# One layer of decoding: whole-matrix loads of wq and w3, and a final copy in two parts

## The chip, the cores and the metric

The kernel runs on one core of one Trainium2 chip. The metric is the device time of one execution in microseconds (us). A core has five engines that concern us: TensorE (PE; its weight loads are shown as PEld), VectorE (DVE), ScalarE (ACT), GpSimd (POOL) and SyncE (SP), each with an instruction stream of its own, and 16 DMA engines that move data between HBM and the on-chip memory SBUF. PSUM is the memory into which TensorE writes its products. An instruction that needs another engine's result, or a transfer, waits on a semaphore, and what stands behind it in the same stream waits with it.

## The reference

One token for each of 4 sequences passes through attention over a cached window and a gated feed-forward block, both with a residual and a layernorm in front:

```
x: 4 x 1024;  wq: 1024 x 4096;  wo: 4096 x 1024
k, v: the last 2048 positions of 4 sequences x 4 heads x 8192 positions x 128
w1, w3: 1024 x 3584;  w2: 3584 x 1024         (all bfloat16)

q   = layernorm(x) @ wq                       # 32 query heads, 8 to each k/v head
p   = softmax(q k^T / sqrt(128));  o = p v
h   = x + o @ wo
out = h + (silu(layernorm(h) @ w1) * (layernorm(h) @ w3)) @ w2
```

Nearly all of the work is reading weights and cache once: the profile counts 55.59 MB read from HBM.

## The kernel before, in words

All weights and the cache pass through one tile, `ring` (line 88), of 160 KiB in each of the 128 partitions. It is no ring of equal slots: a list, `plan` (lines 110 to 125), gives for each load its kind, its function and the address at which it is put. Addresses are written in KiB. `load_rows` (line 90) loads some rows of a weight matrix with one DMA (a wq row takes 8 KiB in a partition, a wo or w2 row 2 KiB, a w1 or w3 row 7 KiB), `load_kv` (line 96) two sequences of k or v with one DMA each. All of these DMAs go out on SyncE's queue.

`load_next(n)` (line 129) takes the next n entries of the plan, issues their DMAs at that place of the program, and puts the resulting views into `loaded`, from which the matmuls take them. The framework sees the program in this order. A load waits for those reads of its address range that stand before it in the program, and a read waits for the last load of its range that stands before it. Which plan entry a call of `load_next` issues therefore depends only on how many entries were taken by the calls ahead of it. Before the change the calls issue:

| call, line | entries | KiB in the tile |
|---|---|---|
| start, 138 | wq rows 0 to 3; wq rows 4 to 7; k 0, 1; k 2, 3; v 0, 1 | 0-32; 32-64; 64-96; 96-128; 128-160 |
| in the q loop at kc = 3, 223 | v 2, 3 | 0-32 |
| in the scores, half of the units, 275 | wo (32 rows) | 32-96 |
| in the p v loop at b = 1, 334 | w1 (8 rows) | 96-152 |
| in the p v loop at b = 3, 334 | w3 rows 0 to 3 | 0-28 |
| in the wo loop at i = 11, 361 | w3 rows 4 to 7 | 28-56 |
| after the wo loop, 362 | w2, 17 rows | 56-90 |
| in the w1 loop at k = 3, 411 | w2, 7, 3 and 1 rows | 90-104; 104-110; 110-112 |

The stages follow each other in the program:

- x is loaded (line 137), normalised and transposed. The q product (lines 210 to 221) runs 64 matmuls (L215), 8 for each of 8 wq rows.
- Scores: keys are transposed on TensorE (L263), copied by VectorE and ScalarE in turn (L267, L269), and multiplied with q (L248). Softmax, then the product with v (L326).
- The wo product (L353): 32 rows, 4 matmuls each, into `y_ps`. Residual and layernorm on VectorE (L366 to L391), with a small matmul for the sums over partitions (L375). `y2_ps` is begun with the residual (L395).
- `gate_up` (line 398) multiplies with w1 into `g_ps` and with w3 into `u_ps` (both L403, 64 matmuls each). Between the two stand the exponential on ScalarE (L415) and add, reciprocal and product on VectorE (L416 to L419), which make the gate `gs`.
- `hg` (L422) is gate times `u_ps`; it is transposed (L425) and multiplied with w2's 28 rows, 4 matmuls each, into `y2_ps` (L433).
- The tail: one copy from PSUM (L443) and one store (L444), both on ScalarE.

The framework's scheduler may exchange neighbouring independent instructions on an engine; within that the engines follow the program.

Of the kernel before, what the change touches and what calls it, by code (L numbers as in the profile page):

```python
# [10 lines left out]
P = 128  # L11
# [8 lines left out]
def kernel(  # L20
# [13 lines left out]
    nc = tc.nc  # L34

    B, _, D = A_x.shape
# [12 lines left out]
    x_flat = A_x.flatten_outer_dims()  # L49
    out_flat = out.flatten_outer_dims()  # L50
# [14 lines left out]
    JG = 4  # L65
    QD = P // JG
    RS = QD // B
# [13 lines left out]
    RQ = 4  # L81
    BS = 2
    wq_v = A_wq.rearrange("(p i) n -> p (i n)", i=KC)
    wo_v = A_wo.rearrange("(p i) n -> p (i n)", i=IO)
    w1_v = B_w1.rearrange("(p i) n -> p (i n)", i=KC)
    w3_v = B_w3.rearrange("(p i) n -> p (i n)", i=KC)
# [9 lines left out]
    def load_kv(at, src, b):  # L96
# [11 lines left out]
    N_Q, N_F = Hq * Dh, F  # L108
    KIB = 512
    plan = [  # L110
        ("wq", load_rows, (0, wq_v, N_Q, 0, 4)),
        ("wq", load_rows, (32 * KIB, wq_v, N_Q, 4, 4)),
        ("k", load_kv, (64 * KIB, A_k_cache, 0)),
        ("k", load_kv, (96 * KIB, A_k_cache, 2)),
        ("v", load_kv, (128 * KIB, A_v_cache, 0)),
        ("v", load_kv, (0, A_v_cache, 2)),
        ("wo", load_rows, (32 * KIB, wo_v, D, 0, 32)),
        ("w1", load_rows, (96 * KIB, w1_v, N_F, 0, 8)),
        ("w3", load_rows, (0, w3_v, N_F, 0, 4)),
        ("w3", load_rows, (28 * KIB, w3_v, N_F, 4, 4)),  # L120
        ("w2", load_rows, (56 * KIB, w2_v, D, 0, 17)),
        ("w2", load_rows, (90 * KIB, w2_v, D, 17, 7)),
        ("w2", load_rows, (104 * KIB, w2_v, D, 24, 3)),
# [5 lines left out]
    def load_next(n=1):  # L129
        for _ in range(n):  # L130
            if cursor[0] < len(plan):
                kind, f, args = plan[cursor[0]]
                loaded.setdefault(kind, []).extend(f(*args))
                cursor[0] += 1

    x_sb = act.tile([B, D], BF16)
    nc.scalar.dma_start(out=x_sb[:], in_=x_flat)
    load_next(5)

    ident = const.tile([P, P], BF16)  # L140
    make_identity(nc, ident[:])
# [5 lines left out]
    for j in range(JG):  # L147
        nc.scalar.dma_start(
            out=x_q[QD * j : QD * (j + 1) : RS, :], in_=x_flat[:, j * CG : (j + 1) * CG]
# [7 lines left out]
    for c in range(2):  # L157
# [8 lines left out]
        out=xn[:], in0=x_sb[:], scalar1=mv[:, 0:1], scalar2=rstd[:, 0:1],  # L166
# [4 lines left out]
    for kc in range(KC):  # L171
# [15 lines left out]
        out=perm[:].rearrange("p (h dq) -> p h dq", dq=JG),  # L187
        in_=ident[:].rearrange("p (dq h) -> p h dq", dq=JG),
# [12 lines left out]
    for j in range(2, JG):  # L201
        nc.vector.tensor_tensor(
            out=same[:, 0, :], in0=same[:, 0, :], in1=ident[:, j * QD : (j + 1) * QD], op=ALU.add
# [6 lines left out]
    for kc in range(KC):  # L210
        wq_t = loaded["wq"][kc]
        for hf in range(CQ // 512):
            for g in range(JG):
                c0 = g * CQ + hf * 512
                nc.tensor.matmul(  # L215
                    q_ps[QD * g : QD * g + B, hf * 512 : (hf + 1) * 512],
                    lhsT=xnT[:, kc, :],
                    rhs=wq_t[:, c0 : c0 + 512],
                    start=(kc == 0),
                    stop=(kc == KC - 1),  # L220
                )
        if kc == RQ - 1:
            load_next()
    q_sb = act.tile([P, CQ], BF16)
    nc.vector.tensor_single_scalar(out=q_sb[:, :512], in_=q_ps[:, :512], scalar=qscale, op=ALU.mult)  # L225
    nc.scalar.mul(out=q_sb[:, 512:], in_=q_ps[:, 512:], mul=qscale)
# [1 line left out]
    for r in range(REP):  # L228
        nc.tensor.transpose(out=qt_ps[:, r, :], in_=q_sb[:, r * Dh : (r + 1) * Dh], identity=ident[:])
    nc.vector.tensor_copy(  # L230
        out=qz[:, :, : Hkv * QD].rearrange("p b (g z) -> p b g z", g=Hkv)[:, :, :, :REP],
        in_=qt_ps[:].rearrange("p r (g x) -> p x g r", g=Hkv)[:, :B, :, :],
# [24 lines left out]
    for u, (b, n) in enumerate(units):  # L257
        k_v = loaded["k"][b]
        kT = ktpool.tile([P, NJ, P], BF16, tag="kT")
        for t in range(NJ // TB):  # L260
            kt_ps = psA.tile([P, TB, P], BF16, tag=f"kt{nt % 4}")
            for jj in range(TB):
                nc.tensor.transpose(  # L263
                    out=kt_ps[:, jj, :], in_=k_v[:, n * NJ + t * TB + jj, :], identity=ident[:]
# [21 lines left out]
        out=Pm[:], in_=scores_ps[:], func=ACT.Exp, bias=nmax[:], scale=1.0, accum_out=rsum[:]  # L286
# [6 lines left out]
    for c in range(NSB):  # L293
# [4 lines left out]
        for g in range(Hkv):  # L298
            if g % 2 == 0:
                nc.vector.tensor_scalar(  # L300
                    out=z[:, :, g, :], in0=pt_ps[:], scalar1=mask[:, g : g + 1], scalar2=None, op0=ALU.mult
# [10 lines left out]
        out=Dm[:], in0=ident[:].rearrange("p (g b r) -> p b g r", g=Hkv, b=B),  # L312
# [35 lines left out]
    y2_ps = psB.tile([P, CG], FP32, tag="y2")  # L348
    g_ps = psB.tile([P, 2, 512], FP32, tag="g")
    u_ps = psB.tile([P, 2, 512], FP32, tag="u")  # L350
    for i in range(IO):
# [34 lines left out]
        out=hn[:], in0=h1[:], scalar1=tot[:, 0:1], scalar2=rstd2[:, 0:1],  # L386
# [5 lines left out]
        out=hnT[:].rearrange("p k x -> p (k x)"), in_=hn[:].rearrange("q (c k) -> q k c", k=KC)  # L392
# [5 lines left out]
    def gate_up(kind, out_ps):  # L398
# [27 lines left out]
        out=hgT[:].rearrange("p i x -> p (i x)"),  # L426
        in_=hg[:].rearrange("q s c -> q (s c)").rearrange("q (c i) -> q i c", i=IF),
# [12 lines left out]
            )  # L440

    res = act.tile([P, CG], BF16)
    nc.scalar.copy(out=res[:], in_=y2_ps[:])  # L443
    nc.scalar.dma_start(out=out_flat.rearrange("b (j c) -> j b c", j=JG), in_=res[0:P:RS, :])  # L444


# [28 lines left out]
```

## Time and profile before

| what | value |
|---|---|
| median of 3 runs | 138.12 us (138.05 to 138.14) |
| the profiled execution's own time | 138.12 us |
| its span, first to last instruction | 136.3 us |
| TensorE matmul busy | 67.9 us (50%) |
| VectorE busy | 42.6 us (31%) |
| ScalarE busy | 31.0 us (23%) |
| SyncE's DMA queue: bytes, share of 16 engines' time | 55.58 MB, 95.3% |
| mean rate | 409 GB/s |
| mean granted TensorE clock | 0.792 of full speed |

Busy time of an engine is the sum of its instructions' durations; shares are of the span. The profile's slices cut the span into 40 equal parts of 3.4 us; each digit is the busy share in tenths. The chain of waits starts at the last instruction and goes back, at each step to what released it. A line of the timeline gives start, length, engine, line of the kernel, operation, output and inputs, a count where several are merged, and in brackets how long the engine stood idle before and what ended that. "SPq" and "ACTq" are instructions that issue a DMA or wait, on the engine's queue. The profile cuts the names `w1`, `w3` and `w2` to `w`, and `y_ps` stands for `y2_ps` too.

### The profile page before, as it was taken

The numbers are of one execution on the slowest core, as the hardware profiler recorded it, in microseconds if no ns is written. First come the engines' busy times: TensorE is split into PE (matmuls) and PEld (weight loads), VectorE is DVE, ScalarE is ACT, GpSimd is POOL, SyncE is SP. The second block draws the span as 40 slices with busy tenths as digits, with TensorE's granted clock in tenths as the row PEclk, the third lists the DMA queues.
The fourth block names the chain that finished last, engine by engine and source line by source line (L and its number), as shares of the span: only waits on it lengthen the run. The fifth ranks groups of instructions, "written<-read, shape, count | busy, mean of one in ns | idle before, by whom it ended". The sixth has DMA issues, their size and how long they took to land.

```text
span 136.3 us, 2302 instructions
## 1 busy us (share of the span) xinstructions
PE 67.9 (50%) x1035; PEld 42.9 (31%) x1035; DVE 42.6 (31%) x73; ACT 31.0 (23%) x36; POOL 1.7 (1%) x8
## 2 busy tenths in 40 slices
PE   0101803698989889105259538830096440900960
PEld 0100201274656565001149427610043210300840
DVE  6440000244444444609940030160000695070000
ACT  0400000155555646092944000000003300000001
POOL 5000000000000000000000000000000000000000
PEclk9999999999999999965555865897557777555577
DMA  5999899999999999997988989989799999989960
GB/s 156 462 462 443 385 413 418 423 447 423 428 437 409 437 437 423 435 582 341 538 385 365 524 365 442 459 353 522 328 412 463 434 437 447 429 388 409 426 261 5
DMA packets 2662, 55.75 MB, mean 409 GB/s; under 512 B 312, under 2 KB 344, under 8 KB 604
## 3 DMA queue, kind: packets, MB, share of 16 engines
q1 hardware_dynamic: 2592, 55.58, 95.3%
q8 instruction: 8, 0.13, 0.3%
q10 hardware_dynamic: 60, 0.02, 0.1%
q14 instruction: 2, 0.02, 0.0%
HBM read 55.59 MB, written 0.01 MB: 408 GB/s over the span
## 4 chain that ended last, share of the span: by engine, by line
DMA 58%; PE 21%; ACT 13%; DVE 5%; issue 1%; SPq 0%; ACTq 0%
DMA ring<-in_B_w_dram 42%; DMA ring<-in_A_wq_dram 16%; PE kt_ps L263 9%; ACT kT L269 6%; PE scores_ps L248 5%; ACT z L304 3%; PE q_ps L215 2%; PE g_ps L403 2%; DVE rmax L280 2%; ACT Pm L285 2%; PE OT_ps L326 2%; DVE pT L294 1%; DVE z L300 1%; ACT L285 1%; DVE q_sb L225 1%
## 5 line engine op out<-in xcount | busy, mean ns | idle before, releaser
L269 ACT COPY kT<-kt_ps 128x1024 bf16<-128x1024 bf16 x16 | 15.8, 1014 | 12.0 <-PE kt_ps L263 12.0
L263 PE MATMUL kt_ps<-ident,ring 128*128 128x128 bf16 x256 | 16.4, 219 | 0.0
L263 PEld LDWEIGHTS <-ring 128*128 128x128 bf16 x256 | 14.3, 98 | 5.0 <-issue 4.9
L267 DVE COPY kT<-kt_ps 128x1024 bf16<-128x1024 bf16 x16 | 11.1, 691 | 15.2 <-PE kt_ps L263 15.2
L215 PE MATMUL q_ps<-ring,xnT 128*4 128x512 bf16 x64 | 6.7, 596 | 12.0 <-DMA ring<-in_A_wq_dram 12.0
L403 PEld LDWEIGHTS <-hnT 128*32 128x32 bf16 x128 | 5.3, 137 | 23.1 <-issue 20.5
L248 PE MATMUL scores_ps<-kT,qz 128*32 128x512 bf16 x64 | 9.9, 609 | 3.1 <-ACT kT L269 3.1
L326 PE MATMUL OT_ps<-z,ring 128*128 128x32 bf16 x256 | 7.4, 185 | 6.7 <-ACT z L304 5.0
L403 PE MATMUL u_ps<-ring,hnT 128*32 128x448 bf16 x64 | 6.3, 572 | 8.3 <-DMA ring<-in_B_w_dram 8.3
L403 PE MATMUL g_ps<-ring,hnT 128*32 128x448 bf16 x64 | 5.4, 525 | 9.0 <-DMA ring<-in_B_w_dram 9.0
L433 PE MATMUL y_ps<-ring,hgT 128*32 128x256 bf16 x112 | 5.7, 370 | 8.4 <-DMA ring<-in_B_w_dram 8.3
L326 PEld LDWEIGHTS <-ring 128*128 128x128 bf16 x256 | 7.3, 103 | 7.4 <-issue 7.4
L433 PEld LDWEIGHTS <-hgT 128*32 128x32 bf16 x112 | 4.4, 129 | 10.3 <-issue 6.1
L215 PEld LDWEIGHTS <-xnT 128*4 128x4 bf16 x64 | 2.1, 116 | 16.2 <-issue 15.9
L353 PE MATMUL y_ps<-ring,o 128*32 128x256 bf16 x128 | 5.8, 365 | 2.0 <-DMA ring<-in_A_wo_dram 2.0
L443 ACT CAST res<-y_ps 128x256 bf16<-128x256 f32 x1 | 0.4, 372 | 26.5 <-PE y_ps L433 26.5
L304 ACT ACTIVATE z<-pt_ps,mask 128x512 bf16<-128x512 f32 x8 | 5.3, 687 | 3.5 <-DVE z L300 3.5
L225 DVE TENSOR_SCALAR q_sb<-q_ps 128x512 bf16<-128x512 f32 x1 | 0.7, 690 | 17.2 <-PE q_ps L215 17.2
L353 PEld LDWEIGHTS <-o 128*32 128x32 bf16 x128 | 4.8, 130 | 3.8 <-issue 3.1
L300 DVE TENSOR_SCALAR z<-pt_ps,mask 128x512 bf16<-128x512 f32 x8 | 5.5, 740 | 1.2 <-ACT z L304 0.8
L296 PE MATMUL pt_ps<-pT,perm 128*128 128x512 bf16 x4 | 2.4, 607 | 6.8 <-DVE pT L294 6.8
L417 DVE RECIPROCAL eg<-eg 128x896 f32<-128x896 f32 x1 | 5.8, 5753 | 0.0
(73 smaller groups left out, 40.5 us busy)
## 6 DMA issues: line engine op xcount, KB each, us to landing
ring<-in_A_wq_dram SPq DMA_DIRECT2D x2, 4096.0 KB, 16.8
ring<-in_A_k_cache_dram SPq DMA_DIRECT2D x4, 2048.0 KB, 25.5
ring<-in_A_v_cache_dram SPq DMA_DIRECT2D x4, 2048.0 KB, 40.2
ring<-in_B_w_dram SPq DMA_DIRECT2D x1, 7168.0 KB
ring<-in_B_w_dram SPq DMA_DIRECT2D x2, 3584.0 KB, 28.6
ring<-in_B_w_dram SPq DMA_DIRECT2D x1, 4352.0 KB
ring<-in_B_w_dram SPq DMA_DIRECT2D x1, 1792.0 KB
ring<-in_B_w_dram SPq DMA_DIRECT2D x1, 768.0 KB
```

Source lines behind the costliest of these rows:

```text
L215: nc.tensor.matmul(q_ps[QD * g : QD * g + B, hf * 512 : (hf + 1) * 512], lhsT=xnT[:, kc, :], rhs=wq_t[:, c0 : c0 + 512], start=(kc == 0), ...
L248: nc.tensor.matmul(scores_ps[QD * g : QD * (g + 1), n * 512 : (n + 1) * 512], lhsT=qz[:, b, g * QD : (g + 1) * QD], rhs=kT_v[:, g, :, :], ...
L263: nc.tensor.transpose(out=kt_ps[:, jj, :], in_=k_v[:, n * NJ + t * TB + jj, :], identity=ident[:])
L267: nc.vector.tensor_copy(out=kT[:, t * TB : (t + 1) * TB, :], in_=kt_ps[:])
L269: nc.scalar.copy(out=kT[:, t * TB : (t + 1) * TB, :], in_=kt_ps[:])
L300: nc.vector.tensor_scalar(out=z[:, :, g, :], in0=pt_ps[:], scalar1=mask[:, g : g + 1], scalar2=None, op0=ALU.mult)
L304: nc.scalar.mul(out=z[:, :, g, :], in_=pt_ps[:], mul=mask[:, g : g + 1])
L326: nc.tensor.matmul(OT_ps[:, b, :], lhsT=loaded["v"][b][:, j, :], rhs=PTz[j // NJ][:, (j % NJ) * B + b, :, :], start=(j == 0), stop=(j == J ...
L353: nc.tensor.matmul(y_ps[QD * j : QD * (j + 1), :], lhsT=o4[:, i, :, :].rearrange("p b s -> p (b s)"), rhs=loaded["wo"][i][:, j * CG : (j + ...
L403: nc.tensor.matmul(out_ps[QD * j : QD * (j + 1), hf, :HF], lhsT=hnT[:, k, :], rhs=loaded[kind][k][:, c0 : c0 + HF], start=(k == 0), stop=( ...
L417: nc.vector.reciprocal(out=eg[:], in_=eg[:])
L433: nc.tensor.matmul(y2_ps[QD * j : QD * (j + 1), :], lhsT=hgT[:, i, :], rhs=loaded["w2"][i][:, j * CG : (j + 1) * CG], start=False, stop=(i ...
```

## The change

wq and w3 become one plan entry, and so one DMA, each. The first call of `load_next` takes 4 entries instead of 5, the call inside the q loop moves behind it, and the other calls stay where they are. The load of x is split into two halves by columns. The final copy is split: VectorE copies columns 0 to 159 and SyncE's queue stores them, ScalarE copies columns 160 to 255 and stores them from its own queue.

```diff
     plan = [
-        ("wq", load_rows, (0, wq_v, N_Q, 0, 4)),
-        ("wq", load_rows, (32 * KIB, wq_v, N_Q, 4, 4)),
+        ("wq", load_rows, (0, wq_v, N_Q, 0, 8)),
         ("k", load_kv, (64 * KIB, A_k_cache, 0)),
         ("k", load_kv, (96 * KIB, A_k_cache, 2)),
         ("v", load_kv, (128 * KIB, A_v_cache, 0)),
         ("v", load_kv, (0, A_v_cache, 2)),
         ("wo", load_rows, (32 * KIB, wo_v, D, 0, 32)),
         ("w1", load_rows, (96 * KIB, w1_v, N_F, 0, 8)),
-        ("w3", load_rows, (0, w3_v, N_F, 0, 4)),
-        ("w3", load_rows, (28 * KIB, w3_v, N_F, 4, 4)),
+        ("w3", load_rows, (0, w3_v, N_F, 0, 8)),
         ("w2", load_rows, (56 * KIB, w2_v, D, 0, 17)),
...
     x_sb = act.tile([B, D], BF16)
-    nc.scalar.dma_start(out=x_sb[:], in_=x_flat)
-    load_next(5)
+    for c0, c1 in ((0, 512), (512, D)):
+        nc.scalar.dma_start(out=x_sb[:, c0:c1], in_=x_flat[:, c0:c1])
+    load_next(4)
...
-        if kc == RQ - 1:
-            load_next()
+    load_next()
...
     res = act.tile([P, CG], BF16)
-    nc.scalar.copy(out=res[:], in_=y2_ps[:])
-    nc.scalar.dma_start(out=out_flat.rearrange("b (j c) -> j b c", j=JG), in_=res[0:P:RS, :])
+    out_v = out_flat.rearrange("b (j c) -> j b c", j=JG)
+    CV = 160
+    nc.vector.tensor_copy(out=res[:, :CV], in_=y2_ps[:, :CV])
+    nc.scalar.copy(out=res[:, CV:], in_=y2_ps[:, CV:])
+    nc.sync.dma_start(out=out_v[:, :, :CV], in_=res[0:P:RS, :CV])
+    nc.scalar.dma_start(out=out_v[:, :, CV:], in_=res[0:P:RS, CV:])
```

## The prediction

> **What bounds the kernel now.** I read the row of DMA slices first, then the chain of waits, then the timeline of the second half, then the sync engine's queue alone. The page's row says that the transfers never pause between start and end:
>
> ```profile
> DMA  5999899999999999997988989989799999989960
> ```
>
> The chain in order of time says which transfers the end hangs on (start, length, what):
>
> ```profile
> 1.16 21.35 DMA ring<-in_A_wq_dram
> ...
> 73.22 25.79 DMA ring<-in_B_w_dram
> ...
> 101.59 31.37 DMA ring<-in_B_w_dram
> ...
> 133.01 0.32 PE y_ps L433 x4
> ...
> 133.35 0.37 ACT res L443
> ```
>
> The timeline shows TensorE starting each product when its weights land (start, length, idle before, releaser in brackets):
>
> ```profile
> 82.25 5.76 PE L353 MATMUL y_ps<-ring,o 128*32 128x256 bf16 x128 [2.04 <-DMA ring<-in_A_wo_dram]
> ...
> 99.06 5.44 PE L403 MATMUL g_ps<-ring,hnT 128*32 128x448 bf16 x64 [9.01 <-DMA ring<-in_B_w_dram]
> ...
> 107.50 3.13 PE L403 MATMUL u_ps<-ring,hnT 128*32 128x448 bf16 x32 [3.00 <-DMA ring<-in_B_w_dram]
> ...
> 115.98 3.17 PE L403 MATMUL u_ps<-ring,hnT 128*32 128x448 bf16 x32 [5.34 <-DMA ring<-in_B_w_dram]
> ...
> 126.30 3.82 PE L433 MATMUL y_ps<-ring,hgT 128*32 128x256 bf16 x68 [7.14 <-DMA ring<-in_B_w_dram]
> 130.55 1.11 PE L433 MATMUL y_ps<-ring,hgT 128*32 128x256 bf16 x28 [0.43 <-DMA ring<-in_B_w_dram]
> 132.38 0.92 PE L433 MATMUL y_ps<-ring,hgT 128*32 128x256 bf16 x16 [0.71 <-DMA ring<-in_B_w_dram]
> ```
>
> So the landings are wo 82.2, w1 99.06, w3 107.50 and 115.98, w2 126.30, 130.55, 132.38, 133.01. 7.34 MB of w1 in 16.8 us is 437 GB/s: one unbroken stream. It stays unbroken because each issue waits only for a read that is done before the stream is empty; the sync queue's issues are
>
> ```profile
> 73.22 0.33 SPq L93 DMA_DIRECT2D ring<-in_B_w_dram  x1
> ...
> 78.84 0.33 SPq L93 DMA_DIRECT2D ring<-in_B_w_dram  x1
> ...
> 85.04 0.33 SPq L93 DMA_DIRECT2D ring<-in_B_w_dram  x1
> ...
> 87.73 0.33 SPq L93 DMA_DIRECT2D ring<-in_B_w_dram  x1
> ```
>
> that is w1, both halves of w3 and the 17 rows of w2, then the three short w2 pieces at 100.7 to 101.6, all well before 126.3.
>
> **What the Trainium skill says.** "DMA: Bandwidth & Descriptors", section "Anatomy of one DMA": the DMA engines don't wait on semaphores; the issuing sequencer waits, before it issues, and everything after it in its stream waits too. The trace agrees: the second half of w3 is issued at 85.04, only when wo's rows have been read. "TensorE: Matmul & The Clock Gate", section "What's actually happening": after some 3.4 us idle the array runs at half rate until about 3.4 us of work have passed. The trace agrees: w2's first 68 matmuls take 56 ns each, the next 28 take 40. "PSUM — Partial Sum Buffer", section "Terms": ScalarE and VectorE must not use one bank's quadrant together. No line of before shows that; it bears on the split copy.
>
> **The change, part by part.**
>
> *What is handed out when.* The calls that issue loads take the next plan entry. Up to w1 the two removed items cancel (one wq entry less, the first call takes 4 instead of 5). w3 then is one entry, so each later entry comes one call early: all of w3 at b = 3, ahead of the wo loop; w2's 17 rows at i = 11 of that loop; w2's 7 rows after it, ahead of w1's loop. The ranges overlap: w3 takes 0 to 56 KiB, wo's rows 0 to 11 lie in 32 to 56 and rows 12 to 28 in 56 to 90, exactly where w2's 17 rows go; w2's 7 rows (90 to 104) cover w1's row 0 and the start of row 1. A load that stands ahead of a read of its range in the program is taken as what is read. So the reads wait for the later load. The compiled order has it:
>
> ```
> L351 Ldweights o4_130 [waits DMAHW7,DMAHW1,DVE]
> L351 Matmult y_ps<-ring,o4_130 32x256 [waits DMAHW2]     (row 12)
> L401 Ldweights hnT [waits DMAHW3]                        (first g_ps)
> ```
>
> Before, the first of them waited for semaphore 7 (wo) alone and the other two had no such wait. The eight semaphores go round in order of issue: 1 is w3, 2 the 17 rows, 3 the 7 rows. (In this part the changed kernel multiplies with w3's and w2's bytes in place of wo's rows 0 to 28, and with w2's in part of w1's rows 0 and 1; number and shapes of the matmuls stay.)
>
> *wq as one DMA.* The first 32 q matmuls (3.58 us at 13.05) no longer run while the second half comes: all 64 start at 22.55. That delays the scores by up to 3.2 us, less what the compiled order gets back by transposing keys ahead of q. v's second half is issued near 29, with some 9 MB still queued (wq, k and v's first half are 21 MB, and 409 GB/s, the page's mean, moves about 11.5 by then). w1 is issued near 76 instead of 73.22, and the stream holds until wo lands at 82.2: hidden. If it came after 79.4 (82.2 less the start-up below) the stream would break, one for one. k's third load waits for wq's semaphore until 22.5, when two k loads are still queued. Cost 0.
>
> *The x load in two.* One more issue of up to 0.57 us on ScalarE's queue; q's inputs were ready at 7.2 and wait for wq till 22.55. Cost 0.
>
> *The stream from wo on.* w3 is issued when wo lands, 82.2 (its new wait), w2's 17 rows right behind; w1 covers both until 99.06. So w1 lands at 99.06, w3 at 115.98, the 17 rows at 126.30, as before. Now TensorE comes after them:
> - 115.98: wo's rows 0 to 11, 48 matmuls, 2 to 2.7 us; then row 12 waits for 126.30. Queued behind it is all of the rest of TensorE's work, and for that DVE's layernorm.
> - 126.30: 80 matmuls, cold. 61 x 56 ns make the first 3.4 us; the warm price is (5.76 - 3.4) / 67 = 35 ns from L353 and 40 from w2's 28: I take 37, 19 x 37 = 0.7. Ends at 130.4.
> - The sync queue holds w2's 7 rows until wo's last rows are read, 130.4: the stream is empty from 126.3. Start-up: wq's first half landed 12.32 us after its issue at 0.73, the second 9.5 after the first, so 2.8; plus 4.25 for the bytes (126.30 to 130.55). Landing: 137.45. The fixed cost of about 2 us that the same DMA section gives is the lower end.
> - Layernorm: y's end at 88.01 to the next product's weights at 92.32, 4.31: 134.7.
> - The compiled order puts 37 u matmuls first: 34 cold at 99 ns (3.17 / 32), 3 warm: 3.6, to 138.3. The wait for the 7 rows has passed by then.
> - g: 64 at the warm price (5.44 - 3.4) / 30 = 68 ns: 4.35, to 142.65. The other 27 u are hidden behind what follows; so are w2's last pieces, issued when w1's rows 1 and 2 are read, near 139.
> - g's end to gs's end: 104.50 to 114.45, 9.95 (table load 1.28, exponential 0.92, add 0.63, reciprocal 5.75, product 1.09). Before, this lay under w3's transfer; now nothing covers it. 152.6.
> - hg and its transpose: 119.20 to 122.08, 2.9: 155.5.
> - w2: 112 matmuls, nothing to wait for: 61 x 56 + 51 x 38 = 5.35: 160.85.
>
> *The tail.* Before, y's end to the span's end is 136.3 - 133.33 = 2.97. The compiled order makes ScalarE's part wait for VectorE's. VectorE's 160 columns: 0.29 for 128 (L336) and 0.42 for 256 (L366), so 0.32; ScalarE's 96: 0.19 for 128 (L320), so about 0.15, and two hand-overs. The later store is issued 0.57 after y instead of 0.42: +0.15. Two smaller stores may gain 0.3 or cost 0.5.
>
> Sum: 160.85 + 3.12 = 164.0 of span. The profiled execution was 138.12 us with a span of 136.3; the 1.82 around it stays: 165.8. The median shown is 138.12 as well.
>
> **The rivals.**
> - *The new waits are already met* (a semaphore counts an earlier load): then only the tail is left, 138.12 + 0.15 = 138.3, not slower by what can be told here. For it: the order shows no counts. Against: semaphores 1 and 2 were used by k in both kernels, and only the changed one waits. It decides if y starts at about 82. 4%.
> - *Only w3 is waited for*, the 17 rows not: y 115.98 to 121.75, layernorm to 126.05, the 7 rows land unbroken at 130.55, g to 135.0, then 9.95 + 2.9 + 5.35 + 3.12 + 1.82: 158.1. Against: the separate wait at row 12. 3%.
> - *The clock stays cold* in y, u, g and w2: +0.4, +2.05, +0.9: 169.2. For it: in 116 to 119.2 and 119.2 to 126.3 the granted clock was 0.50. Against: L353 and L403 did speed up midway. 8%.
> - *Warm throughout*: y -1.1, g -0.85 (then the 7 rows' landing holds it), w2 -1.1: 162.8. Long idle times stand against it. 3%.
>
> **How the numbers follow.** 82% for 165.8, with 164 to 168.8 of its own (clock phases, start-up 2.0 to 3.5, tail). Range 163.8 to 169.2. Slower by over 0.2% (about what a measurement of this kernel can tell from none) 96%, same 3%, faster 1%.
>
> **What would show it.** y's matmuls starting near 116 and pausing until 126; a hole of some 7 us in the DMA row after 126 with the 7 rows issued at 130; the reciprocal on the chain; a second half that ends on engines, not on DMA. A y that starts at 82, or a stream that still runs until 133, would make the forecast wrong.

## The result, and the profile after

The changed kernel takes 166.44 us (median of 6 runs, 165.73 to 167.3) against 138.13 (138.05 to 138.3) of the kernel before: a ratio of 1.2056, 95% interval 1.2017 to 1.2095. The profiled execution took 166.42 us with a span of 164.6. It is not the same layer any more: TensorE runs matmuls of the same number and shapes, but nowhere multiplies with wo's rows 0 to 28 or with a part of w1's rows 0 and 1.

The row of DMA slices of the changed kernel's page, each slice now 4.1 us, is no longer full to the end:

```profile
DMA  7998979999999999899899999999991280700000
```

Up to slice 30 it looks as before. Slices 31 and 32 are nearly empty, slices 33 and 35 are filled once more, and after slice 35 nothing moves: over the last eighth of the span engines work alone. The same bytes are moved, 55.75 MB, but at a mean of 339 GB/s over the span instead of 409. The chain of waits, in order of time (start, length, what), says what the end now hangs on:

```profile
41.31 41.10 DMA ring<-in_A_wo_dram
...
82.87 43.56 DMA ring<-in_B_w_dram
...
126.48 3.85 PE y_ps L351 x79
...
134.60 3.91 PE u_ps L401 x28
138.52 3.73 PE g_ps L401 x47
...
145.22 5.76 DVE eg L415
...
155.15 5.73 PE y_ps L431 x58
...
161.26 0.24 ACT res L444
```

Before, a DMA stood on this chain until 132.97. Now the last DMA on it ends at 126.44 (w2's 17 rows), and what it releases is the second part of the wo product. After it come the rest of that product, layernorm, the products with w3 and w1, the reciprocal and w2's product, one after the other, for 38 us. The timeline of the changed kernel shows where TensorE stood until then:

```profile
82.81 0.27 PE L339 MATMUL o_ps<-oT,perm 128*128 128x128 bf16 x1 [0.73 <-DVE oT L337]
...
116.28 2.75 PE L351 MATMUL y_ps<-ring,o 128*32 128x256 bf16 x48 [33.21 <-issue]
...
126.48 3.82 PE L351 MATMUL y_ps<-ring,o 128*32 128x256 bf16 x80 [7.44 <-DMA ring<-in_B_w_dram]
...
134.60 3.91 PE L401 MATMUL u_ps<-ring,hnT 128*32 128x448 bf16 x37 [2.27 <-DVE hnT L389]
137.94 4.27 PE L401 MATMUL g_ps<-ring,hnT 128*32 128x448 bf16 x64
...
155.15 5.69 PE L431 MATMUL y_ps<-ring,hgT 128*32 128x256 bf16 x112 [11.80 <-DVE hgT L423]
```

wo's product, one run of 128 at 82.25 before, is now cut into 48 and 80, at row 12, and starts at 116.28, where the second half of w3 landed before (115.98). The first wait of 33.2 us is put down to "issue": the semaphores are waited for by the weight load in front of the matmul, and the profile names no releaser there. The second is named as a DMA of a feed-forward weight. Of the three that the wo product could wait for, w3 must have landed by 116.28 and w2's 7 rows were not issued before 130.34, so it is w2's 17 rows. The sync engine's queue shows these issues:

```profile
82.50 0.80 SPq L93 DMA_DIRECT2D ring<-in_B_w_dram  x2
...
130.34 0.33 SPq L93 DMA_DIRECT2D ring<-in_B_w_dram  x1
...
140.00 0.80 SPq L93 DMA_DIRECT2D ring<-in_B_w_dram  x2
```

w3 and the 17 rows go out together when wo lands; the 7 rows go out when wo's product is done. In between the stream stands still. The same stretch before and after (the figures are the length, the busy time and number of instructions of TensorE's matmuls and weight loads, VectorE, ScalarE and GpSimd, the granted TensorE clock, the busy share of the DMA engines, and GB/s):

```profile
126.30:130.50 4.20, 3.82 (x68) 3.04 (x68) 0.00 (x0) 0.00 (x0) 0.00 (x0) 0.50 0.98 416
126.30:130.50 4.20, 3.82 (x80) 3.06 (x79) 0.10 (x1) 0.00 (x0) 0.00 (x0) 0.62 0.01 4
```

### The profile page after: what moved, and what is told of

It reads as the page before. It is cut to its first block, busy times and chain, and to the rows that moved or that the text cites. A ratio compares the mean times of both kernels' runs of the same rounds, so it can differ in the third digit from the quotient of the medians.

```text
span 164.6 us, 2303 instructions
## 1 busy us (share of the span) xinstructions
PE 65.3 (40%) x1035; PEld 41.4 (25%) x1035; DVE 42.8 (26%) x74; ACT 31.0 (19%) x36; POOL 1.7 (1%) x8
## 2 busy tenths in 40 slices
DMA packets 2402, 55.75 MB, mean 339 GB/s; under 512 B 320, under 2 KB 344, under 8 KB 600
## 4 chain that ended last, share of the span: by engine, by line
DMA 65%; PE 20%; DVE 8%; ACT 3%; issue 1%; SPq 0%; DVEq 0%; ACTq 0%
DMA ring<-in_B_w_dram 26%; DMA ring<-in_A_wo_dram 25%; DMA ring<-in_A_wq_dram 13%; PE kt_ps L261 4%; DVE eg L415 4%; PE q_ps L214 3%; PE y_ps L431 3%; PE u_ps L401 2%; PE y_ps L351 2%; PE g_ps L401 2%; ACT kT L267 2%; PE scores_ps L246 2%; DVE hgT L423 1%; ACT L413 1%; DVE hg L420 1%
## 5 line engine op out<-in xcount | busy, mean ns | idle before, releaser
L351 PE MATMUL y_ps<-ring,o 128*32 128x256 bf16 x128 | 6.6, 391 | 40.7 <-issue 33.2
L261 PE MATMUL kt_ps<-ident,ring 128*128 128x128 bf16 x256 | 17.1, 220 | 0.0
L246 PE MATMUL scores_ps<-kT,qz 128*32 128x512 bf16 x64 | 10.5, 609 | 2.6 <-ACT kT L267 2.6
L214 PE MATMUL q_ps<-ring,xnT 128*4 128x512 bf16 x64 | 5.7, 538 | 9.4 <-DMA ring<-in_A_wq_dram 9.4
L401 PE MATMUL u_ps<-ring,hnT 128*32 128x448 bf16 x64 | 5.4, 483 | 2.3 <-DVE hnT L389 2.3
L401 PEld LDWEIGHTS <-hnT 128*32 128x32 bf16 x128 | 4.0, 119 | 6.6 <-issue 2.9
L171 PE MATMUL tp_ps<-ident,xn 4*128 4x4 bf16 x8 | 0.7, 199 | 12.7 <-DVE xn L164 12.7
```

Of the source, the lines that this page charges most:

```text
L214: nc.tensor.matmul(q_ps[QD * g : QD * g + B, hf * 512 : (hf + 1) * 512], lhsT=xnT[:, kc, :], rhs=wq_t[:, c0 : c0 + 512], start=(kc == 0), ...
L246: nc.tensor.matmul(scores_ps[QD * g : QD * (g + 1), n * 512 : (n + 1) * 512], lhsT=qz[:, b, g * QD : (g + 1) * QD], rhs=kT_v[:, g, :, :], ...
L261: nc.tensor.transpose(out=kt_ps[:, jj, :], in_=k_v[:, n * NJ + t * TB + jj, :], identity=ident[:])
L351: nc.tensor.matmul(y_ps[QD * j : QD * (j + 1), :], lhsT=o4[:, i, :, :].rearrange("p b s -> p (b s)"), rhs=loaded["wo"][i][:, j * CG : (j + ...
L401: nc.tensor.matmul(out_ps[QD * j : QD * (j + 1), hf, :HF], lhsT=hnT[:, k, :], rhs=loaded[kind][k][:, c0 : c0 + HF], start=(k == 0), stop=( ...
```

## The experiments

Each timed run stands beside runs of the kernel before on the same chip (138.14 us median; 138.23 for the two runs with x alone and wq alone). The ratios can differ by 0.1% from the quotient of the medians, so a tenth of a us between two runs says little.

**Where the 28 us are: w3 in a place where nothing is overwritten.** The changed kernel, with one call taken out:

```diff
-        if b % BS == BS - 1:
+        if b == BS - 1:
             load_next()
```

> The changed kernel without the call of load_next at b = 3, so that w3 (still one DMA) is issued at i = 11 of the wo loop and all of w2 where the kernel before had it; nothing is loaded over rows that are still to be read. Theory (the 28 us come from reads that wait for a load handed out one call early): w3 lands near 116, its 64 matmuls end near 121.5 instead of 119.2, hg and its transpose near 124.4, still ahead of w2's landing at 126.3; the stream runs unbroken to 133 and only the new tail is left: 138.3 to 139.0 us. Rival (a matrix as one DMA costs time in itself, since its matmuls start only at the end): at least the 3.2 us of half of w3's matmuls on top, 141 us or more, or a stream slower than 430 GB/s.

138.89 us, ratio 1.0043 (1.0031 to 1.0055). The timeline shows all 64 matmuls of w3 after the one landing, and w2's product still waiting for its own transfer:

```profile
116.14 5.80 PE L401 MATMUL u_ps<-ring,hnT 128*32 128x448 bf16 x64 [11.28 <-DMA ring<-in_B_w_dram]
121.99 1.09 DVE L420 TENSOR_TENSOR hg<-u_ps,gs 128x896 bf16<-128x896 f32 x1 [7.18 <-PE u_ps L401]
123.11 1.70 DVE L423 STREAM_TRANSPOSE hgT<-hg 128x896 bf16<-128x896 bf16 x1
...
126.40 3.82 PE L431 MATMUL y_ps<-ring,hgT 128*32 128x256 bf16 x68 [4.46 <-DMA ring<-in_B_w_dram]
```

The later matmuls shorten the last idle time from 7.14 to 4.46 us and cost nothing. So one large DMA is not what is slow; the place of its issue in the program is. That is shown, since this kernel has every other edit of the change and loses 0.75 us by the medians (0.6 by the ratio), not 28.3.

**The other way round: w3 alone.** The kernel before, with

```diff
-        ("w3", load_rows, (0, w3_v, N_F, 0, 4)),
-        ("w3", load_rows, (28 * KIB, w3_v, N_F, 4, 4)),
+        ("w3", load_rows, (0, w3_v, N_F, 0, 8)),
```

> The kernel before with w3 as one plan entry and nothing else; wo's rows 0 to 28 and part of w1's rows 0 and 1 are then multiplied as w3's and w2's bytes, as in the changed kernel. Theory: this entry alone makes the whole loss: 166.44 less what the new tail costs (0.15 to 0.75), so 165.7 to 166.3. Rival (wq's single DMA and the later v loads have a share, by way of the scores 2 to 3 us later): below 165.

166.13 us, ratio 1.2003 (1.1974 to 1.2033), inside the range of the theory: the one entry makes the loss, and the timeline repeats that of the changed kernel.

```profile
116.10 2.75 PE L352 MATMUL y_ps<-ring,o 128*32 128x256 bf16 x48 [33.23 <-issue]
126.31 4.42 PE L352 MATMUL y_ps<-ring,o 128*32 128x256 bf16 x80 [7.47 <-DMA ring<-in_B_w_dram]
```

wq is still in two DMAs here, so its edit has no share that can be seen.

**Two waits or one.** The changed kernel without the call at i = 11, so that w3 stays early and w2 returns to its old calls:

```diff
-        if i == 11:
-            load_next()
```

> The changed kernel without the call at i = 11: w3 is still issued ahead of the wo loop (wo's rows 0 to 11 are multiplied as w3's bytes), w2's pieces where the kernel before had them. It parts the loss in two. Theory: y waits for w3 alone, 116.3 to 122; the 17 rows are issued when wo's last rows are read, 121.5, and land at 121.5 + 2.8 + 10.3 = 134.6, after a hole of 5 to 8 us; layernorm to 126.3, g to 131.8, its gate to 141.7, hg and transpose to 144.6, w2's product 5.7 to 150.3, tail 3.7, 1.8 around it: 155.8 us, so that w3's place costs some 17.5 us and the place of w2's first two entries 10.6. Rival (one wait makes the whole loss): 164 to 167.

154.51 us (median of three runs, 153.43 to 154.75; with the fourth, the profiled one at 156.13, it is 154.63), ratio 1.1162 (1.1125 to 1.12). wo's product is one run again:

```profile
116.24 6.43 PE L351 MATMUL y_ps<-ring,o 128*32 128x256 bf16 x128 [33.66 <-DMA ring<-in_B_w_dram]
```

Here the profile does name the DMA. So of the 28.3 us, w3's place makes about 16 (154.51 - 138.14 = 16.4), and the place of w2's first two entries, on top of it, the other 12. The forecast of this run, 155.8, was 1.3 too high. In the profiled execution, the slowest of the four, wo's product ends at 122.7 instead of 122.0 and the gate is ready at 142.7 instead of 141.7; w2's product then takes 5.0 us instead of 5.7, and the span ends 0.4 later than expected. Which step is shorter in the other three was not traced.

**The tail.** The kernel before with the new tail alone, the last block of the change's diff:

> The kernel before with the split copy and the two stores alone. By the forecast's tail term: +0.15 us, 138.3. By the changed kernel's trace, where y's end to the span's end took 3.72 us instead of 2.97: +0.75, 138.9. A gain (the copy is shorter, two queues) would give 137.9 or less.

138.51 us, ratio 1.0024 (1.0017 to 1.003): +0.37 us, between the two figures. The timeline shows the copies one after the other, as the compiled order had it; first the kernel before, then this run:

```profile
133.35 0.37 ACT L443 CAST res<-y_ps 128x256 bf16<-128x256 f32 x1 [26.54 <-PE y_ps L433]
133.75 0.61 ACTq L444 DMA_DIRECT2D out_dram<-res  x1
...
133.31 0.33 DVE L445 CAST res<-y_ps 128x160 bf16<-128x160 f32 x1 [11.48 <-PE y_ps L433]
133.67 0.69 SPq L447 DMA_DIRECT2D out_dram<-res  x1
133.67 0.24 ACT L446 CAST res<-y_ps 128x96 bf16<-128x96 f32 x1 [26.20 <-DVE res L445]
133.94 0.61 ACTq L448 DMA_DIRECT2D out_dram<-res  x1
```

Together they take 0.60 us from 133.31, where ScalarE's single copy took 0.37. Two more runs take the tail apart. First the two copies and one store of all columns:

> The kernel before with the copy split as in the change, but one store of all columns from ScalarE's queue. If the copies, one after the other, are what the tail costs: as the whole tail, 138.4 to 138.5. If the second store is: 138.1 to 138.2.

138.43 us, ratio 1.0022 (1.0012 to 1.0032). Its store is issued at 133.98, 0.23 later than that of the kernel before. Then the one copy and two stores:

> The kernel before with its one copy on ScalarE, but the two stores of 160 and 96 columns from SyncE's and ScalarE's queue. If the second store costs: 138.4 to 138.6. If the serial copies do: 138.1 to 138.2. A gain from two queues: below 138.0.

138.52 us, ratio 1.003 (1.002 to 1.004). Each half alone comes out slower by about as much as both together: 0.29 and 0.38 alone, 0.37 together, each known to about 0.1 us. In the run with one copy and two stores both stores start at once:

```profile
133.32 0.37 ACT L445 CAST res<-y_ps 128x256 bf16<-128x256 f32 x1 [26.56 <-PE y_ps L433]
133.72 0.69 SPq L446 DMA_DIRECT2D out_dram<-res  x1
133.73 0.61 ACTq L447 DMA_DIRECT2D out_dram<-res  x1
```

Its span ends at 136.7, so 2.97 us after the later issue, against 136.3 - 133.75 = 2.55 for the single store of the kernel before. One profiled execution each doesn't settle what a second store costs: over the seven kernels here with a single store the same time is 2.55 to 2.88 us, over the five with two stores 2.66 to 2.97. So the 0.23 us of the serial copies is seen in the traces; a cost of the second store rests on the timed runs, and its cause was not looked for (pieces of 320 and 192 bytes in place of 512, or the second queue).

**wq, and the x load.** The kernel before with the blocks of the change's diff that touch wq, the load of x and the calls `load_next(4)` and `load_next()` behind the q loop:

> The kernel before with wq as one DMA, the call of load_next moved behind the q loop, and the x load in two; w3 and the tail as before. Theory: q starts at 22.8 instead of 13.05 and the scores run 2 us later, but the stream does not notice: 138.1 +- 0.3. Rival: the later issues of v and w1 break the stream or the second x half holds q up: the delay of 2 us shows, 140.

138.42 us, ratio 1.0011 (1.0002 to 1.0019), 0.02 above the range expected and far from the rival's 140. q's product takes place after wq's one landing, and the kernel hardly notices:

```profile
22.68 5.82 PE L215 MATMUL q_ps<-ring,xnT 128*4 128x512 bf16 x64 [9.53 <-DMA ring<-in_A_wq_dram]
...
99.18 4.70 PE L402 MATMUL g_ps<-ring,hnT 128*32 128x448 bf16 x64 [7.60 <-DMA ring<-in_B_w_dram]
```

w1 lands at 99.18 instead of 99.06: the delay of about 2 us in the scores does not reach the stream. To see whose the last 0.1 to 0.3 us is, each half of the edit by itself:

> The kernel before with the x load in two halves by columns and nothing else. It asks what the 0.1 to 0.3 us of the run with wq and x come from, and whether the second half lands late here too (in the changed kernel the second BN statistics waited 6.8 us for it, until 10.6). If the extra DMA at the start delays the stream: 138.3 to 138.5, with wq's first landing 0.1 to 0.3 later. If wq's single DMA does: 138.1 to 138.2. A second half as late as there leaves q's inputs ready near 13.5, 0.5 after wq's first half, and hidden, since q's second half starts at 22.55.

> The kernel before with wq as one DMA and the call of load_next moved behind the q loop; x, w3 and the tail as before. If wq's single DMA delays the stream: 138.3 to 138.5. If the x halves do: 138.1 to 138.2, though q's product still starts at 22.7.

138.40 us, ratio 1.0016 (1.0008 to 1.0023), with x in halves; 138.39, ratio 1.0008 (1.0 to 1.0017), with wq as one DMA. These are at the limit of what can be told, and the two can't be ranked: neither is more than about 0.3 us. In the profiled execution with wq as one DMA the stream itself is 0.3 late (wq is used at 22.82 instead of 22.55, w1 at 99.38 instead of 99.06); with x in halves it is not (wq's first half at 12.98 instead of 13.05, the last product ends at 133.34 as before), and the 0.2 us by which its span is longer lie behind the issue of the store, which the edit doesn't touch. What can be seen is x's second half arriving late; first the kernel before, then x in halves alone:

```profile
2.52 1.27 DVE L158 BATCH_NORM_STATS2 stats<-x_sb 4x6 f32<-4x512 bf16 x2
...
2.40 0.62 DVE L159 BATCH_NORM_STATS2 stats<-x_sb 4x6 f32<-4x512 bf16 x1
7.89 0.68 DVE L159 BATCH_NORM_STATS2 stats<-x_sb 4x6 f32<-4x512 bf16 x1 [4.86 <-DMA x_sb<-in_A_x_dram]
```

**Whole-matrix loads in a safe order with the old tail.** The changed kernel with w3 at i = 11 (the first experiment's edit) and the kernel before's copy and store:

> The changed kernel with w3 at i = 11 (as e1) and the kernel before's tail: whole-matrix loads of wq and w3 in a safe order and nothing else. If the new tail is what e1 loses: 138.1 to 138.4. If one large w3 load costs on top: 138.7 or more.

138.45 us, ratio 1.002 (1.0011 to 1.0029), between the two ranges that were named. With the new tail the same edits took 138.89 on another chip, so the tail makes roughly 0.3 to 0.45 of the 0.75 and the loads some 0.3. No arrangement tried beats the kernel before. Its last bytes land at 133.0 at the end of an unbroken stream, and none of these edits makes the stream shorter.

A word of caution on all differences under half a microsecond: every edit other than the early loads, whatever it touched, came out 0.1 to 0.6 us slower by the ratios. No edit that should change nothing was run, so how much of each is due to the edit is not known.

## Why the prediction was right

It named 165.8 us and 166.44 were measured. The mechanism is the one that it gave: reads that wait for loads handed out one call early, and hidden work that comes to lie behind the stream. The steps can be set beside the trace:

| step | forecast | measured |
|---|---|---|
| wo's product starts; goes on at row 12 | 115.98; 126.30 | 116.28; 126.48 |
| wo's product ends, and the 7 rows are issued | 130.4 | 130.34 |
| first matmul after layernorm | 134.7 | 134.60 |
| g's first matmul starts, after 37 of u | 138.3 | 137.94 |
| g ends | 142.65 | 142.25 |
| gate ready | 152.6 | 152.17 |
| w2's product starts, ends | 155.5, 160.85 | 155.15, 160.88 |
| tail to the end of the span | 3.12 | 3.72 |
| span | 164.0 | 164.6 |

- *What is handed out when* carried the whole forecast. The run with w3 as one entry alone (166.13) and the run that takes out one call (138.89) show both directions.
- *The stream from wo on*: the steps that repeat a stage of before on the same engine came within 0.1 us (layernorm 4.31 forecast, 4.26 measured). Those whose price depends on TensorE's clock were off by up to 0.4, in both directions: wo's 80 matmuls took 3.85 instead of 4.1, the 37 of u 3.34 instead of 3.6, w2's 112 took 5.73 instead of 5.35. That w2's product still ends within 0.03 us of the forecast is luck, as these errors offset each other.
- *The cold phase of TensorE* (the time at half clock when a product begins) was taken to last 3.4 us, after the page that the prediction cites, and the kernel before was read as agreeing. The traces don't agree with that length. In slices of 0.1 us the granted clock in the kernel before is 0.50 for 4.3, 4.6, 3.0 and 4.6 us from the start of wo's product, w1's, the first half of w3's and w2's. In the changed kernel it is 3.0 us for wo's last 80 matmuls, 5.1 from u's start and 5.1 in w2's product. With 4.6 instead of 3.4 us, the sum that gave 68 ns for a warm matmul gives about 47, an estimate: 46 cold ones at 99 ns fit into 4.6 us, and (5.44 - 4.6) / 18 is left for each of the others. Too short a cold phase and too dear a warm matmul came from one slip, and so nearly cancelled in u and g. In w2's product they didn't. The rivals of an always cold and an always warm clock are both refuted: in the changed kernel wo's product, g and w2's product all change to the full clock on their way.
- *The landing of the 7 rows* was to be 137.45, after a pause of some 7 us. In slices of 0.25 us the 17 rows' bytes are through at 125.0, the first bytes of the 7 rows move at 131.25, 0.9 us after the issue, and the last before 136.5. g follows u without a gap at 137.94, so the landing lies between these two times, and was not what the end waited for. The 2 us that the prediction gave as the lower end of the start-up stand in the section it cites for transfers issued by GpSimd; these go out from SyncE.
- *The tail* is the term that was mis-sized: +0.15 forecast, +0.75 in the changed kernel's trace. Half of it lies before the later store, which is issued 0.78 us after the end of w2's product instead of 0.42 (0.57 was forecast), the other half behind it, 2.94 us to the end of the span instead of 2.55:

```profile
160.90 0.32 DVE L443 CAST res<-y_ps 128x160 bf16<-128x160 f32 x1 [5.80 <-PE y_ps L431]
...
161.66 0.62 ACTq L446 DMA_DIRECT2D out_dram<-res  x1
```

- The second store was given a chance to gain 0.3 or to cost 0.5 and was put at nothing. Alone, with one copy, it came out 0.38 slower; by the traces its share stays open.
- *wq and x at no cost*: right to within 0.3 us. v's last load was issued by 26.9 (forecast near 29) and w1 at 75.17 (near 76). That x's second half is used only at 10.63 was not foreseen; it stayed hidden, since wq was waited for until 22.77.
- *The other rivals*: that the new waits are already met is refuted by y's start at 116.28; that only w3 is waited for, by the pause at row 12. Its forecast of 158.1 is not that of the two-wait experiment, where w2's 17 rows are issued later too.

When a DMA stream sets the end, TensorE's pace hardly shows; once its stages follow each other it does. In the traces w2's 112 matmuls take 4.99 us in the two-wait run, 5.73 in the changed kernel and 5.88 with w3 alone, after cold phases of 3.6, 5.1 and 5.4 us, and all of it lies on the chain. Whether this is why single runs of the changed kernel lie 1.6 us apart, and those of the kernel before 0.25, is not shown: the fastest of the six has the lowest mean granted clock, 0.725.

## What to carry to other kernels

Where loads are handed out from a list by calls placed in the program, two entries made into one move every later load one call forward, unless a call is taken out with them, as was done for wq and not for w3; check for each load whether its address range is still to be read at the new place, because a framework that goes by program order then makes the old data's readers wait for the new data, and read it. In a kernel bound by a transfer stream, the time between a landing and its use is free only while the stream runs on: a load that is issued after a late reader turns all of that hidden work into the critical path at once. Splitting a small final copy and store over two engines gained nothing here: the copies ran in turn, and two stores were no faster than one.

## What was not expected of the hardware

Two loads of 4 KB each were issued one behind the other from 0.74 us on ScalarE's queue, beside large loads. In the run with only that edit the first was used at 2.40 us and the second at 7.89; in the five kernels that also have wq as one DMA the second was used at 10.34 to 10.63. The single load of 8 KB in the kernel before was used at 2.52. Small DMAs beside a running stream can arrive microseconds apart. Why, no run here shows.

TensorE's granted clock stayed at half speed for anything from 3.0 to 5.8 us after a product began, in the four kernels of which the slices were read (the kernel before, the changed one, w3 alone, the two-wait run). A forecast that gives it one length can be off by 2 us.
